# Retention and bilinear feed-forward on one core: weight pieces of 2, 3, 3 and 4 blocks, shared K^T V banks, first rows by thirds, one stretch moved

## The chip, the cores and the metric

The kernel runs on one core of a Trainium2 chip. The metric is the device time of one execution in microseconds (us), the median of several runs; lower is better. A profiled execution gives a trace beside it: PE is TensorE (matmul), PEld its weight load, DVE is VectorE, ACT is ScalarE, POOL is GpSimd, SP is SyncE, which issues most of the DMAs. L12 is line 12 of the kernel's file.

## What is computed

Retention over q, k, v (8 batches, 8 heads, 576 positions, 64 per head), with a decay gamma per head, and after it a bilinear feed-forward on the 4608 tokens, all in float32 outside of the chip:

```python
scores = scale * np.matmul(q, k.transpose(0, 1, 3, 2))
Dmat = np.where(rel >= 0, gamma[:, None, None] ** rel[None, :, :], 0.0)
attn = np.matmul(scores * Dmat[None], v)                  # B, H, S, D
x = attn.transpose(0, 2, 1, 3).reshape(B * S, H * D)      # 4608 x 512
out = ((x @ w_a) * (x @ w_b)) @ w_out                     # 512 -> 1536 -> 512
```

## The kernel before

**Retention in blocks of 64.** The tokens are handled in 18 pairs `n` of 256 tokens (the last 64 positions of each batch are gathered into two pairs of their own). Within a block of 64 positions, K Q^T is formed on PE ("scores", `sc`), masked to the causal part on DVE (`sT`) and multiplied with V ("keys"). What comes from earlier blocks goes through a state K^T V per head, summed over blocks: PE forms `kv`, DVE adds it up in `sums`, ACT converts the sums to bf16 `states`, and PE multiplies these with Q. The output `o` times the decay `qs` is `x`, written by DVE in bf16.

**Opening.** The first three pairs are handled in six steps (batch, half of the heads): step 0 and 2 make pair 0, steps 1 and 3 make pair 1, steps 4 and 5 (later) pair 2. A step casts Q and K to bf16 (`cast_step`, on an engine that is named), decays V (`values_step`), transposes Q and K on PE (`transpose_step`), forms scores (`score_step`) and K^T V (`state_step`: `state_products` on PE, then `state_copies` on ACT: `state_after`, which the second 128 tokens need, and the sums `own` and `second`, kept for later), and its output (`open_step`, `step_states`, `step_keys`, `close_step`; the last is the DVE product that writes x). The order is written out by hand in lines 858 to 934: each engine works through its own instructions in the order in which they stand there. PE fills waits with matmuls of ones (`warm`), which keep nothing.

**Weights.** `load_w` has POOL's queue cast columns of wa and wb from float32 to bf16 while loading them. `WCOLS` gives the pieces in blocks F of 128 columns, 3, 4 and 5 of the 12; wo follows in three thirds (`load_wo`). SP's later loads of q, k, v stand behind a small DMA (`gate`) that reads the first third of wo.

**Feed-forward.** `ffn_block` takes 512, 256, 256 and then 512 tokens at a time. For each F, four matmuls give `pa` (x wa), ACT copies it to `ha` in bf16, four give `pb` (x wb), and DVE multiplies the two into `hT`. In the first block the F are grouped as the weight pieces are: all pa of a piece, then all pb. The first piece's pa is begun early by `ffn_begin` on the first 256 tokens and by `begin_with` on the next. Then, for every 128 tokens u, twelve matmuls with wo give the rows `po`, which ACT or DVE copies to `osb`, and SP stores them; for the first three blocks the stores are held back (`held`).

**Banks.** `ps_ffn` is a pool of four PSUM banks with the tag "ab", shared by pa, pb, po, the transposes of the opening and two `kv` tiles of a stretch. A new tile waits for the last reader of the bank that it takes.

**Work in between.** `ffn_block` is a generator that yields a cost for each matmul (512 columns are 1). A list `todo` holds functions with due costs; the loop in lines 1029 to 1037 runs those that are due at the next edge (after a pb; after the 4th, 8th and 12th matmul of a row group). Block 0 runs from cost 0 to 144, block 1 to 216 (its two row groups from 192 and 204), block 2 to 288. `stretch(into, outof)` is such a function: it puts on PE the states part of pair `outof`, K^T V and the scores of pair `into`, and the keys of `outof`; an ACT copy `fence` stands between the first and the last. What follows on DVE and ACT is put on the list `later`: the adds of `sums` (in two parts for pairs in `SPLIT`), the two halves of x (`scaled`), and two entries that convert the sums on ACT (`convert`, `convert_swapped`) and mask the scores on DVE (`masked`). `pop()` in `ffn_block` issues one entry: after each pb, and in a row group after matmul 3, 6, 9 and at its end behind the `osb` copy. `flush()` at a block's end issues what is left, before the next block's first instruction. Each engine runs its instructions in the order of issue.

Of the kernel before, what the change touches and what calls it, by code (L numbers as in the profile page):

```python
# [18 lines left out]
def kernel(  # L19
# [25 lines left out]
    NP = NTOK // 256  # L45
    LEFT = {NP - 3: 0, NP - 1: 1}
    FIRST = 3
    SPLIT = (3, 5)
    assert S == 9 * 64 and B == 8

    PAIRS = [(0, 0), (1, 0), (2, 0), (0, 1), (1, 1), (2, 1)]
# [76 lines left out]
    def half(i):  # L128
        return slice(64 * i, 64 * i + 64)
# [132 lines left out]
    def load_w(f0, f1, which="ab"):  # L262
        if "a" in which:
            nc.gpsimd.dma_start(wa_sb[:, :, f0:f1], wa_r[:, :, f0:f1])
        if "b" in which:
            nc.gpsimd.dma_start(wb_sb[:, :, f0:f1], wb_r[:, :, f0:f1])
# [12 lines left out]
    def pop():  # L279
        if later:  # L280
            later.pop(0)()
# [28 lines left out]
    def cast_step(i, w, on):  # L310
        COPY[on](by_parity(natural[STEPS[i]][0][:, w]), given(i, w))  # L311
# [70 lines left out]
    def state_copies(i, kvs, rest=None):  # L382
# [12 lines left out]
        else:  # L395
            rest.append(keep)

    def total_of(n):

        own = own_sums[n]  # L400
        if n < FIRST - 1:
            nc.gpsimd.tensor_tensor(own, own, second[:, n], op=ALU.add)
            nc.gpsimd.tensor_copy(own_states[n], own)
        else:
            nc.vector.tensor_tensor(own, own, second[:, n], op=ALU.add)
            nc.scalar.copy(own_states[n], own)
        sums_of[n, 0] = own
# [266 lines left out]
    def close_outputs(n):  # L674

        o, begun = opened.pop(n)
        keys_into(n, o, begun)
        scaled = scaling(n, o)
        later.append(lambda: scaled(0))
        later.append(lambda: scaled(1))  # L680
# [33 lines left out]
    def stretch(into, outof):  # L714

        flush()
        if into == FIRST:
            ps_next("ps_pair")
        if into in LEFT:
            own = [ps_ffn.tile([128, HP, 2, 64], FP32, tag="ab", name=f"os{a}")  # L720
                   for a in (0, 1)]
            of_keys = ps_o[0].tile([128, 2, HP, 2, 64], FP32, tag="o",
                                   name="o2")
            from_states(outof, own, Begun())
            masked = matched(into)
            keys_into(outof, of_keys, Begun())
            summing(outof, own, of_keys)
            later.append(lambda: masked(0))
            later.append(lambda: masked(1))
            return  # L730
        if outof is not None:
            open_outputs(outof)
        convert, convert_swapped = keyed(into, outof is None)
        masked = matched(into)
        if outof is not None:
            close_outputs(outof)
        later.append(lambda: (convert(), masked(0)))
        later.append(lambda: (convert_swapped(), masked(1)))

    WCOLS = [3, 4, 5]  # L740

    def store(u, cols, osb):
        n, u = place(u // 2), u % 2
# [25 lines left out]
    def begin_with(F, c, m):  # L769
        begun[F, c, m] = True  # L770
        nc.tensor.matmul(begun[F][:, 256 * m:256 * m + 256],  # L771
                         wa_sb[:, c, F * 128:F * 128 + 128],
                         x_of(256 * m, 256)[:, c], start=(c == m == 0),
                         stop=(c == NC - 1), skip_group_check=True)

    def ffn_block(tb, tok0, n, runs):

        xT = x_of(tok0, n)
        hT = h_pool.tile([128, NF, 512], BF16, tag="h", name="hT")
        f0 = 0  # L780
        for count in runs:
            has = {}
            for F in range(f0, f0 + count):
                fs = slice(F * 128, (F + 1) * 128)
                pa = (begun[F] if tb == 0 and F in begun else
                      ps_ffn.tile([128, 512], FP32, tag="ab", name="pa"))
                for c in range(NC):
                    if tb == 0 and (F, 0, 0) in begun:
                        if (F, c, 1) not in begun:
                            begin_with(F, c, 1)  # L790
                        if c < NC - 1:
                            yield n / 512, False
                        continue
                    nc.tensor.matmul(pa[:, 0:n], wa_sb[:, c, fs],  # L794
                                     xT[:, c],
                                     start=(c == 0), stop=(c == NC - 1))
                    if c < NC - 1:
                        yield n / 512, False
                if n == 512 and tb:
                    pop()  # L800
                ha = ha_pool.tile([128, 512], BF16, tag="ha", name="ha")
                nc.scalar.copy(ha[:, 0:n], pa[:, 0:n])  # L802
                has[F] = ha
                yield n / 512, False
            for F in range(f0, f0 + count):
                fs = slice(F * 128, (F + 1) * 128)
                pb = ps_ffn.tile([128, 512], FP32, tag="ab", name="pb")
                for c in range(NC):
                    nc.tensor.matmul(pb[:, 0:n], wb_sb[:, c, fs],  # L809
                                     xT[:, c],  # L810
                                     start=(c == 0), stop=(c == NC - 1))
                    if c < NC - 1:
                        yield n / 512, False
                nc.vector.tensor_tensor(hT[:, F, 0:n], has[F][:, 0:n],  # L814
                                        pb[:, 0:n], op=ALU.mult)
                pop()
                yield n / 512, True
            f0 += count
        for u in range(n // 128):
            final = tok0 + (u + 1) * 128 == NTOK  # L820
            osb = o_pool.tile([128, DM], FP32, tag="osb", name="osb")
            edges = (0, DM // 2, 3 * DM // 4, DM) if final else (0, DM)
            for part in range(len(edges) - 1):
                cols = slice(edges[part], edges[part + 1])
                po = ps_ffn.tile([128, 512], FP32, tag="ab", name="po")
                width = cols.stop - cols.start
                for F in range(NF):
                    nc.tensor.matmul(po[:, 0:width],  # L828
                                     hT[:, F, u * 128:(u + 1) * 128],
                                     wo_sb[:, F, cols],  # L830
                                     start=(F == 0), stop=(F == NF - 1))
                    if F in (2, 5, 8):
                        pop()
                    if F < NF - 1:
                        yield width / 512, F % 4 == 3
                if n == 256 or (u + part) % 2 == 0:
                    nc.scalar.copy(osb[:, cols], po[:, 0:width])  # L837
                else:
                    nc.vector.tensor_copy(osb[:, cols], po[:, 0:width])  # L839
                if tb < 3:  # L840
                    held.append((tok0 // 128 + u, cols, osb))
                else:
                    store(tok0 // 128 + u, cols, osb)
                pop()
                yield width / 512, True
# [5 lines left out]
    def warm(count, n):  # L851

        w = ps_ffn.tile([128, 512], FP32, tag="ab", name="w")
        for _ in range(count):
            nc.tensor.matmul(w[:, 0:n], ones[:, 0:128], ones[:, 0:n],  # L855
                             start=True, stop=True)

    W1, W2 = 128 * WCOLS[0], 128 * (WCOLS[0] + WCOLS[1])
    vector, pool_ = nc.vector, nc.gpsimd
    warm(8, 512)  # L860
    make_qs(qs_o, 0, 0, 256)
# [18 lines left out]
    warm(2, 512)  # L880
    transpose_step(2, (K, "dve"))
    warm(2, 512)
    load_w(0, W1, "a")
    cast_step(1, Q, "act")
    score_step(2)
    transpose_step(1, (K, "act"))
# [2 lines left out]
    values_step(2, 1, pool_)  # L889
    values_step(2, 0, pool_)  # L890
    make_qs(qs_o, 3, 0, 256)
    load_w(0, W1, "b")
    warm(2, 512)
    score_step(1)
    cast_step(3, Q, "act")
    state_step(2)
    cast_step(3, K, "pool")
    warm(2, 512)
    transpose_step(3, (Q, "act"))
    transpose_step(3, (K, "dve"))  # L900
# [2 lines left out]
        values_step(1, kp, pool_)  # L903
    values_step(3, 0, nc.scalar)
    values_step(3, 1, pool_)
    load_w(W1, W2)
    score_step(3)
    rest = []
    state_step(1, rest)
    state_step(3, rest)  # L910
    for keep in rest:
        keep()
    open_step(1)
    step_keys(1, {0, 1})
    step_states(1, False)
    close_step(1)
    open_step(3, ps_sc)
    step_keys(3, {0, 1})
    step_states(3, False)
    close_step(3)  # L920
    for F in range(3):
        ffn_begin(F)
    for c in (0, 1):
        for F in range(3):
            begin_with(F, c, 1)
    load_w(W2, DFF)
    for i in (0, 1, 2):
        load_wo(i)
    make_masks()
# [54 lines left out]
    def third_turn():  # L984
        for i in (4, 5):
# [6 lines left out]
    todo += [(60 + 10 * n, total_of, (n,)) for n in (0, 1)]  # L992
    todo += [(136, total_of, (2,))]
    todo += [(28 + 6 * step, pair_tables, (step,)) for step in range(13)]
    todo += [(170, stretch, (3, None)), (197, stretch, (4, 3)),
             (252, stretch, (5, 4)), (274, open_alone, (5,)),
             (278, close_outputs, (5,)), (336, stretch, (6, None)),
             (372, stretch, (7, 6)), (408, stretch, (8, 7))]
# [69 lines left out]
```

## Time and profile before

| | us |
|---|---|
| median of 3 runs | 325.16 (325.08 to 325.69) |
| the profiled execution | 325.43 |
| its span, first to last instruction | 323.7 |
| busy: PE, DVE, ACT, POOL | 314.0, 165.4, 131.5, 118.8 |
| first matmul of the feed-forward (L771) starts | 16.81 |
| first rows with wo (L828) start | 37.57 |
| block 1's last rows to block 2's first pa (chain) | 68.61 |
| last PE matmul done (chain) | 320.9 |

The span is that of the profiled execution; what lies around it (325.43 - 323.7) is launch and end. In the timelines each row is start, duration, engine, line, operation, output <- input, shape and count; rows of one form that follow each other are merged. In the chain of waits a row is start, duration and what the end was waiting for.

### The profile page before, as it was taken

The numbers are of one execution on the slowest core, as the hardware profiler recorded it, in microseconds if no ns is written. First come the engines' busy times: TensorE is split into PE (matmuls) and PEld (weight loads), VectorE is DVE, ScalarE is ACT, GpSimd is POOL, SyncE is SP. The second block draws the span as 40 slices with busy tenths as digits, with TensorE's granted clock in tenths as the row PEclk, the third lists the DMA queues.
The fourth block names the chain that finished last, engine by engine and source line by source line (L and its number), as shares of the span: only waits on it lengthen the run. The fifth ranks groups of instructions, "written<-read, shape, count | busy, mean of one in ns | idle before, by whom it ended". The sixth has DMA issues, their size and how long they took to land.

```text
span 323.7 us, 8631 instructions
## 1 busy us (share of the span) xinstructions
PE 314.0 (97%) x3573; PEld 164.4 (51%) x3611; DVE 165.4 (51%) x294; ACT 131.5 (41%) x293; POOL 118.8 (37%) x158
## 2 busy tenths in 40 slices
PE   7899999999999999999999999999999999999996
PEld 3564457778444554444454545454445444444444
DVE  5744445665546754835374626562566256514321
ACT  7735753463435523533253324442433343313321
POOL 4990077574755274447165305450530000000000
PEclk9999999999999999999999999999999999999999
DMA  8999999999999999999999169935840520031013
GB/s 216 255 196 207 259 231 189 200 176 206 174 221 223 195 208 206 269 222 263 175 197 216 52 163 198 207 74 144 194 86 19 104 76 2 2 97 32 1 23 108
DMA packets 145431, 50.90 MB, mean 157 GB/s; under 512 B 126704, under 2 KB 140912, under 8 KB 145392
## 3 DMA queue, kind: packets, MB, share of 16 engines
q1 hardware_dynamic: 140112, 45.37, 68.4%
q0 software_dynamic: 4752, 4.72, 8.8%
q8 instruction: 28, 0.46, 0.6%
q10 hardware_dynamic: 528, 0.26, 0.3%
q14 instruction: 11, 0.09, 0.1%
HBM read 37.75 MB, written 9.44 MB: 146 GB/s over the span
## 4 chain that ended last, share of the span: by engine, by line
PE 92%; DMA 2%; SPq 2%; ACT 1%; issue 1%; DVE 1%; DVEq 0%
PE pb L809 29%; PE po L828 29%; PE pa L794 28%; DMA qf<-in_q_dram 2%; SPq L159 2%; PE sc L600 1%; PE o L628 1%; PE o L641 1%; PE kv L538 1%; PE pa L771 1%; ACT state_after L386 0%; ACT vb L319 0%; PE tp L329 0%; DVE hT L814 0%; ACT own L390 0%
## 5 line engine op out<-in xcount | busy, mean ns | idle before, releaser
L814 DVE TENSOR_TENSOR hT<-ha,pb 128x512 bf16<-128x512 bf16 (+1 forms) x120 | 75.9, 633 | 94.8 <-PE pb L809 86.6
L802 ACT CAST ha<-pa 128x512 bf16<-128x512 f32 (+1 forms) x120 | 64.8, 543 | 115.9 <-PE pa L794 109.9
L809 PE MATMUL pb<-xT,wb_sb 128*128 128x512 bf16 (+1 forms) x474 | 111.2, 357 | 0.5
L794 PE MATMUL pa<-xT,wa_sb 128*128 128x512 bf16 (+1 forms) x452 | 106.9, 356 | 1.2 <-issue 0.6
L828 PE MATMUL po<-wo_sb,hT 128*128 128x512 bf16 (+2 forms) x442 | 94.7, 367 | 1.7 <-issue 1.4
L809 PEld LDWEIGHTS <-wb_sb 128*128 128x128 bf16 x480 | 47.0, 98 | 46.6 <-issue 0.3
L794 PEld LDWEIGHTS <-wa_sb 128*128 128x128 bf16 x468 | 45.0, 98 | 44.4 <-issue 0.2
L828 PEld LDWEIGHTS <-hT 128*128 128x128 bf16 x456 | 42.7, 98 | 47.2
L484 POOL CAST qkb<-qf 64x1024 bf16<-64x1024 f32 x15 | 15.5, 1031 | 64.4 <-DMA qf<-in_q_dram 55.1
L495 POOL TENSOR_TENSOR vb<-vf,vs 128x1024 bf16<-128x1024 f32 (+1 forms) x17 | 28.9, 1700 | 13.3 <-DMA vf<-in_v_dram 6.1
L839 DVE COPY osb<-po 128x512 f32<-128x512 f32 (+2 forms) x17 | 11.1, 653 | 43.0 <-PE po L828 43.0
L837 ACT COPY osb<-po 128x512 f32<-128x512 f32 (+1 forms) x21 | 12.0, 573 | 43.4 <-PE po L828 40.5
L484 POOL CAST qkb<-kf 64x1024 bf16<-64x1024 f32 (+1 forms) x17 | 16.4, 966 | 16.7 <-DMA kf<-in_k_dram 16.5
L563 DVE TENSOR_TENSOR sums<-kv,sums 128x256 f32<-128x256 f32 x44 | 18.7, 424 | 2.8 <-PE kv L538 0.8
L609 DVE TENSOR_TENSOR sT<-sc,mask 128x512 bf16<-128x512 f32 x30 | 19.4, 681 | 0.0
L488 POOL CAST qkb<-kf 64x512 bf16<-64x512 f32 (+1 forms) x34 | 18.7, 579 | 1.0
L488 POOL CAST qkb<-qf 64x512 bf16<-64x512 f32 x30 | 17.6, 615 | 0.6
L567 ACT CAST states<-sums 64x512 bf16<-64x512 f32 x26 | 16.0, 617 | 0.3
L654 DVE TENSOR_TENSOR xT<-o,qs 128x512 bf16<-128x512 f32 x24 | 15.4, 682 | 1.5 <-PE o L641 1.5
L311 POOL CAST qkb<-kf 128x512 bf16<-128x512 f32 x5 | 3.1, 617 | 16.9 <-DMA kf<-in_k_dram 16.9
L355 DVE TENSOR_TENSOR sT<-sc,mask_s 128x1024 bf16<-128x1024 f32 x6 | 7.2, 1222 | 1.3 <-PE sc L347 1.2
L855 PE MATMUL w<-ones 128*128 128x512 bf16 x17 | 6.3, 482 | 1.5 <-DVE idxp_f L204 1.5
(88 smaller groups left out, 163.5 us busy)
## 6 DMA issues: line engine op xcount, KB each, us to landing
qf<-in_q_dram SPq DMA_DIRECT2D x32, 256.0 KB, 4.7
vf<-in_v_dram SPq DMA_DIRECT2D x32, 256.0 KB, 5.2
kf<-in_k_dram SPq DMA_DIRECT2D x31, 256.0 KB, 4.8
out_dram<-osb SPq DMA_DIRECT2D x25, 256.0 KB, 3.2
out_dram<-osb SPq DMA_DIRECT2D x21, 128.0 KB, 2.6
wo_sb<-in_moe_w_out_dram POOLq DMA_DIRECT2D x3, 512.0 KB, 16.7
qf<-in_q_dram SPq DMA_DIRECT2D x8, 128.0 KB, 3.2
kf<-in_k_dram SPq DMA_DIRECT2D x8, 128.0 KB, 3.5
```

What stands on the lines that cost most here:

```text
L484: nc.gpsimd.tensor_copy(qkb[0:64, w, e], t[0:64, e])
L488: nc.gpsimd.tensor_copy(to[:, :, 1 - r], fro[:, :, r])
L495: nc.gpsimd.tensor_tensor(vb[:, e].rearrange("p (h d) -> p h d", d=D), t[:, e].rearrange("p (h d) -> p h d", d=D), decay[:, at], op=ALU.mult)
L563: nc.vector.tensor_tensor(sums[:, i], own, prev, op=ALU.add)
L567: nc.scalar.copy(to(half(1 - r)), fro(half(r)))
L609: nc.vector.tensor_tensor(sT[:, on].rearrange("p c k s -> p (c k) s"), sc[:, on].rearrange("p c k s -> p (c k) s"), mask3.unsqueeze(1).to_ ...
L654: nc.vector.tensor_tensor(x_of(t0, 128).rearrange("p c (a s) -> p c a s", a=2), o[:, :, :, kp].rearrange("p a c s -> p c a s"), qs[:, :, s ...
L794: nc.tensor.matmul(pa[:, 0:n], wa_sb[:, c, fs], xT[:, c], start=(c == 0), stop=(c == NC - 1))
L802: nc.scalar.copy(ha[:, 0:n], pa[:, 0:n])
L809: nc.tensor.matmul(pb[:, 0:n], wb_sb[:, c, fs], xT[:, c], start=(c == 0), stop=(c == NC - 1))
L814: nc.vector.tensor_tensor(hT[:, F, 0:n], has[F][:, 0:n], pb[:, 0:n], op=ALU.mult)
L828: nc.tensor.matmul(po[:, 0:width], hT[:, F, u * 128:(u + 1) * 128], wo_sb[:, F, cols], start=(F == 0), stop=(F == NF - 1))
```

## The change

It does five things. (1) The weights come in pieces of 2, 3, 3 and 4 blocks, so the first block groups its F in this way and begins two of them early instead of three; wa's second piece is issued on POOL right behind wb's first, ahead of the values of steps 1 and 3, and wb's second where both stood. The cast of K in step 3 goes from POOL to DVE, ahead of the mask of step 1. (2) `last_states` forms K^T V of steps 1 and 3 in two shared banks and copies both steps together, four ACT copies instead of eight; the outputs follow as keys, keys, states, states and then both DVE products. (3) `rows_together` forms the first two row groups of block 0 side by side, four blocks of wo at a time. (4) `stretch(4, 3)` is due at cost 201 instead of 197. (5) Pair 4's adds are split in two, and the second part is put behind the two halves of x.

```diff
--- before.py
+++ after.py
@@ -45,7 +45,7 @@
     NP = NTOK // 256
     LEFT = {NP - 3: 0, NP - 1: 1}
     FIRST = 3
-    SPLIT = (3, 5)
+    SPLIT = (3, 4, 5)
     assert S == 9 * 64 and B == 8
 
     PAIRS = [(0, 0), (1, 0), (2, 0), (0, 1), (1, 1), (2, 1)]
@@ -394,6 +394,22 @@
             keep()
         else:
             rest.append(keep)
+
+    def last_states():
+
+        own, later_half = kvs = [
+            ps_ffn.tile([128, 2, 2, 64], FP32, tag="ab", name=f"kv1{a}")
+            for a in (0, 1)]
+        fresh = set(QUADS)
+        for i in (1, 3):
+            state_products(i, [kv[:, i // 2] for kv in kvs], fresh)
+        for r in (0, 1):
+            nc.scalar.copy(state_after[half(r), 1, :, half(r)],
+                           own[half(r)].rearrange("p i j d -> p (i j) d"))
+        nc.scalar.copy(own_sums[1],
+                       own.rearrange("p i j d -> p (i j) d"))
+        nc.scalar.copy(second[:, 1],
+                       later_half.rearrange("p i j d -> p (i j) d"))
 
     def total_of(n):
 
@@ -734,10 +750,12 @@
         masked = matched(into)
         if outof is not None:
             close_outputs(outof)
+        if into == 4:
+            later.append(later.pop(1))
         later.append(lambda: (convert(), masked(0)))
         later.append(lambda: (convert_swapped(), masked(1)))
 
-    WCOLS = [3, 4, 5]
+    WCOLS = [2, 3, 3, 4]
 
     def store(u, cols, osb):
         n, u = place(u // 2), u % 2
@@ -772,6 +790,28 @@
                          wa_sb[:, c, F * 128:F * 128 + 128],
                          x_of(256 * m, 256)[:, c], start=(c == m == 0),
                          stop=(c == NC - 1), skip_group_check=True)
+
+    def rows_together(tok0, hT, us):
+
+        pos = [ps_ffn.tile([128, 512], FP32, tag="ab", name="po") for _ in us]
+        for f0 in range(0, NF, 4):
+            for u, po in zip(us, pos):
+                for F in range(f0, f0 + 4):
+                    nc.tensor.matmul(po, hT[:, F, u * 128:(u + 1) * 128],
+                                     wo_sb[:, F], start=(F == 0),
+                                     stop=(F == NF - 1))
+                    if F < NF - 1:
+                        yield 1, F % 4 == 3
+                pop()
+                if f0 + 4 < NF:
+                    continue
+                osb = o_pool.tile([128, DM], FP32, tag="osb", name="osb")
+                if u % 2 == 0:
+                    nc.scalar.copy(osb, po)
+                else:
+                    nc.vector.tensor_copy(osb, po)
+                held.append((tok0 // 128 + u, slice(0, DM), osb))
+                yield 1, True
 
     def ffn_block(tb, tok0, n, runs):
 
@@ -816,7 +856,9 @@
                 pop()
                 yield n / 512, True
             f0 += count
-        for u in range(n // 128):
+        if tb == 0:
+            yield from rows_together(tok0, hT, (0, 1))
+        for u in range(2 if tb == 0 else 0, n // 128):
             final = tok0 + (u + 1) * 128 == NTOK
             osb = o_pool.tile([128, DM], FP32, tag="osb", name="osb")
             edges = (0, DM // 2, 3 * DM // 4, DM) if final else (0, DM)
@@ -855,7 +897,8 @@
             nc.tensor.matmul(w[:, 0:n], ones[:, 0:128], ones[:, 0:n],
                              start=True, stop=True)
 
-    W1, W2 = 128 * WCOLS[0], 128 * (WCOLS[0] + WCOLS[1])
+    edges = [128 * sum(WCOLS[:i]) for i in range(len(WCOLS) + 1)]
+    pieces = list(zip(edges, edges[1:]))
     vector, pool_ = nc.vector, nc.gpsimd
     warm(8, 512)
     make_qs(qs_o, 0, 0, 256)
@@ -880,7 +923,7 @@
     warm(2, 512)
     transpose_step(2, (K, "dve"))
     warm(2, 512)
-    load_w(0, W1, "a")
+    load_w(*pieces[0], "a")
     cast_step(1, Q, "act")
     score_step(2)
     transpose_step(1, (K, "act"))
@@ -889,12 +932,13 @@
     values_step(2, 1, pool_)
     values_step(2, 0, pool_)
     make_qs(qs_o, 3, 0, 256)
-    load_w(0, W1, "b")
+    load_w(*pieces[0], "b")
+    load_w(*pieces[1], "a")
     warm(2, 512)
+    cast_step(3, K, "dve")
     score_step(1)
     cast_step(3, Q, "act")
     state_step(2)
-    cast_step(3, K, "pool")
     warm(2, 512)
     transpose_step(3, (Q, "act"))
     transpose_step(3, (K, "dve"))
@@ -903,27 +947,23 @@
         values_step(1, kp, pool_)
     values_step(3, 0, nc.scalar)
     values_step(3, 1, pool_)
-    load_w(W1, W2)
+    load_w(*pieces[1], "b")
     score_step(3)
-    rest = []
-    state_step(1, rest)
-    state_step(3, rest)
-    for keep in rest:
-        keep()
-    open_step(1)
-    step_keys(1, {0, 1})
-    step_states(1, False)
-    close_step(1)
-    open_step(3, ps_sc)
-    step_keys(3, {0, 1})
-    step_states(3, False)
-    close_step(3)
-    for F in range(3):
+    last_states()
+    for i, banks in ((1, None), (3, ps_sc)):
+        open_step(i, banks)
+        step_keys(i, {0, 1})
+    for i in (1, 3):
+        step_states(i, False)
+    for i in (1, 3):
+        close_step(i)
+    for F in range(WCOLS[0]):
         ffn_begin(F)
     for c in (0, 1):
-        for F in range(3):
+        for F in range(WCOLS[0]):
             begin_with(F, c, 1)
-    load_w(W2, DFF)
+    for piece in pieces[2:]:
+        load_w(*piece)
     for i in (0, 1, 2):
         load_wo(i)
     make_masks()
@@ -992,7 +1032,7 @@
     todo += [(60 + 10 * n, total_of, (n,)) for n in (0, 1)]
     todo += [(136, total_of, (2,))]
     todo += [(28 + 6 * step, pair_tables, (step,)) for step in range(13)]
-    todo += [(170, stretch, (3, None)), (197, stretch, (4, 3)),
+    todo += [(170, stretch, (3, None)), (201, stretch, (4, 3)),
              (252, stretch, (5, 4)), (274, open_alone, (5,)),
              (278, close_outputs, (5,)), (336, stretch, (6, None)),
              (372, stretch, (7, 6)), (408, stretch, (8, 7))]
```

## The prediction

> **What bounds the kernel.** Read first: the page's engine line, then the chain of waits, then the timelines of the two places that the diff touches (8 to 21 us and 60 to 76 us), then the DMA issues.
>
> ```profile
> PE 314.0 (97%) x3573; PEld 164.4 (51%) x3611; DVE 165.4 (51%) x294; ACT 131.5 (41%) x293; POOL 118.8 (37%) x158
> ```
>
> TensorE is idle 9.7 of 323.7 us. In the table of 1 us windows nearly all of it lies before 16.8 us and in the 2.5 us of last store; from 16.8 us to 320.9 us PE is busy 95 to 100% of almost every window at clock 1.00. The change removes no matmul, so it can gain only by letting the feed-forward start before 16.81 us, and every new wait of PE behind that is paid in full. PE in the opening (start, duration), then ACT and DVE at the same time:
>
> ```profile
> 15.70 0.32 PE L437 MATMUL o<-sT,vb 64*64 64x128 bf16 x9 [0.25 <-issue]
> 15.96 0.28 PE L421 MATMUL o<-qkT,state_after 128*128 128x128 bf16 x2
> 16.17 0.42 PE L437 MATMUL o<-sT,vb 64*64 64x128 bf16 x16
> 16.52 0.29 PE L421 MATMUL o<-qkT,state_after 128*128 128x128 bf16 x2
> 16.81 2.79 PE L771 MATMUL pa<-xT,wa_sb 128*128 128x256 bf16 x24
> ```
> ```profile
> 14.93 1.08 ACT L386 CAST state_after<-kv 64x128 bf16<-64x128 f32 x4
> ```
> ```profile
> 14.64 1.21 DVE L355 TENSOR_TENSOR sT<-sc,mask_s 128x1024 bf16<-128x1024 f32 x1
> ```
>
> The reader should see that step 3's mask ends at 15.85, that L771 follows the last L421 without a gap, and that four state copies end at 16.01. The DMA issues (KB written, us from issue to landing):
>
> ```profile
> wa_sb<-in_moe_w_a_dram POOLq DMA_DIRECT2D x1, 640.0 KB, 10.6
> wb_sb<-in_moe_w_b_dram POOLq DMA_DIRECT2D x1, 640.0 KB, 13.1
> wa_sb<-in_moe_w_a_dram POOLq DMA_DIRECT2D x1, 512.0 KB, 7.0
> wb_sb<-in_moe_w_b_dram POOLq DMA_DIRECT2D x1, 512.0 KB, 8.2
> ...
> wa_sb<-in_moe_w_a_dram POOLq DMA_DIRECT2D x1, 384.0 KB, 7.7
> wb_sb<-in_moe_w_b_dram POOLq DMA_DIRECT2D x1, 384.0 KB, 7.1
> ```
>
> Added to their issues on the POOL timeline (wa 9.07, 14.78, 16.31; wb 11.56, 15.58, 17.05) they land at 16.77, 18.66, 21.78, 23.78, 26.91 and 30.15 us, with 384, 768, 1280, 1792, 2432 and 3072 KB there by then. The first landing also sits at PE's start: the weight load of L771 is shown waiting 0.2 us for it.
>
> **Opening, the pieces.** The first piece is 256 KB instead of 384, so by the stream's 200 KB/us it lands about 0.6 us earlier (near 16.1) and no longer holds PE. For a start S = 16.6, PE needs 512 KB at 18.5 (16 half-width matmuls at 0.116, from 24 in 2.79), 896 KB at 20.2 (8 of L809 at 0.216), 1280 KB at 22.8, 1664 at 25.4, 2048 at 28.0, 2560 at 30.6, 3072 at 34.0. Read off the landings in proportion, these amounts are there at 17.4, 19.4, 21.8, 23.3, 25.0, 27.6 and 30.2. Least slack 0.8 us: cost 0, taken as -0 to +0.4 because the 512 KB piece at 21.78 came 0.6 us behind the proportion. Two more DMA issues on POOL (0.77 each) stand before wo and the masks; with the K cast gone (0.62) POOL ends its opening near 21.9, and the first index table that DVE wants from it is due near 23.7: hidden.
>
> **Opening, the cast and the moved issue.** wa's second piece now stands ahead of step 1's values on POOL: 0.81 in, 0.62 of K cast out, so values shift by under 0.2 us; ACT's own values of step 3 (until 15.04) still end last. DVE is free from 11.50 (x of step 0 written) to 11.88; K of step 3, landing between its neighbours in the SP queue (V of step 2 at 10.43, Q of step 3 at 12.07), about 11.3, costs 0.43 there and pushes the mask of step 1 by about 0.05 us, which nothing reads before 15.13. Cost 0.
>
> **Opening, shared banks.** Eight ACT copies of 128 columns (14.93 to 16.81) become four of 256. They now wait for step 3's products, whose last matmul ends at 15.34. A 128x256 copy out of PSUM is 0.37 us (L802's 256 form), so the two state copies end near 16.1. PE meanwhile does the keys of step 1, then of step 3 (mask done 15.85; 16 matmuls take 0.35 before the next), then all four state matmuls (0.31 in the block of four at 48.06 to 48.37): 15.9 + 0.35 + 0.31 = 16.56 at best. With the 0.25 us issue hole at 15.45 kept, keys of step 1 end at 15.96 and S is 16.62. Against 16.81 that is -0.19 to -0.25; I take **-0.2**, bounds -0.3 (nothing can pass the mask) and 0 (the hole grows, or the x of step 3, due 17.9 and wanted 18.0 now that two blocks are begun instead of three, comes 0.1 to 0.2 late).
>
> **First rows by thirds.** Same 24 matmuls, same banks (four: po, po and two free), copies still one on ACT and one on DVE. The last third of wo lands at 38.1 (issue 19.2 + 18.9), was wanted at 39.3 (37.57 + 8 x 0.216), is now wanted at 40.9. It was not late before: 0. Row 0's copy moves 0.8 us later, and on ACT now precedes the Q cast of step 5, which PE's transposes want at 43.4; done by 42.9, so hidden, bounds 0 to +0.2.
>
> **The later stretch.** Stretch(4, 3), due 197, ran at cost 200, after the 8th matmul of block 1's first rows; due 201 it runs at 204, after the 12th. What it defers is popped at matmuls 3, 6, 9 and the end of a row group. Before: adds and first x half still in rows 0, second x half, then both conversions inside rows 1. Now only four pops are left in rows 1, and with the adds cut in two and the second half put last they are add, x, x, add. The conversions are emitted by the flush behind the block, **behind the copy of rows 1 and ahead of block 2's first ha copy** on ACT. ACT and the chain before:
>
> ```profile
> 66.06 0.59 ACT L837 COPY osb<-po 128x512 f32<-128x512 f32 x1 [1.66 <-PE po L828]
> 66.67 0.41 ACT L570 CAST states<-sums 128x256 bf16<-128x256 f32 x1
> 67.08 1.25 ACT L567 CAST states<-sums 64x512 bf16<-64x512 f32 x2
> 68.34 0.82 ACT L567 CAST left_states<-sums 64x256 bf16<-64x256 f32 x2
> 69.06 0.57 ACT L837 COPY osb<-po 128x512 f32<-128x512 f32 x1
> 69.54 0.84 ACT L802 CAST ha<-pa 128x256 bf16<-128x256 f32 x2
> ```
> ```profile
> 65.21 3.40 PE po L828 x15
> 68.61 0.44 PE pa L794 x4
> ...
> 70.36 0.44 PE pa L794 x4
> ```
>
> DVE stays in time: adds begin 0.86 later (65.45), two adds 0.9, two x halves 1.28, so x is complete near 67.7 as before (66.38 + 1.28) and block 2 can start at 68.65; the last two adds end at 68.5, before pb wants their bank at 68.9. ACT does not. It idles through rows 1, copies them from 68.66 (start to start 0.61), then L570 0.41, L567 1.26, left_states 0.72, all read off the start times above: the first ha begins at 71.66 and ends at 72.03. PE has four banks: pa, pb, pa, pb of block 2 fill them, 4 x 0.44 = 1.75 us, until 70.41; the next pa needs the bank that the first ha copy empties, and every other bank waits behind that copy too (hT reads ha). Before, that copy ended at 69.91, 0.45 ahead of need; now it is 72.05 - 70.4 = **1.65 us** late. Behind it hT, pb and pa follow in step, as ha copies come each 0.47 us against PE's 0.88 a pair. Bounds: 1.3 (each of the spacings 0.07 shorter) to 2.0 (hT's turn and the wake-up add to it). Nothing later gives it back: PE has no idle time that waits on absolute time (DMA) behind this point.
>
> **Sum.** 325.43 is the profiled execution's time with span 323.7 in it; -0.2 + 1.65 = +1.45 gives span 325.15 and 326.9 for that execution. The median of the runs shown is 325.16, 0.27 below it, so **326.6**. The likeliest case's own range, by its bounds: 326.1 to 327.3.
>
> **Rivals.**
> (a) *Not slower*: ACT's queue is not what PE waits for. It would take conversions issued inside rows 1, or under 1.35 us of them in front of the first ha, so that it ends before 70.4. For: ACT is 41% busy and before had 0.45 us to spare. Against: the emission order and its one queue. Then only the opening counts: 325.16 - 0.2 = 324.95, at most 324.85.
> (b) *Half a stall*: the copies run closer together and the next bank is free sooner, say half of 1.65: 325.8. Against: their start times are back to back already.
> (c) *The stream falls behind*: each of the two pieces added holds the weights up by as much as a 384 KB piece took (18.66 - 16.77 = 1.9 us): the last third of wo lands at 41.9 against 40.9, 1.0 more: 327.6. Against: time per KB is 1.89/384, 3.13/640 and 3.24/640, 4.9 to 5.1 ns for every size, which leaves no fixed part. The Trainium skill, page "DMA: Bandwidth & Descriptors", section "Rules for kernel authors", speaks against the cut: it wants transfers of 1 MiB or more, and "Anatomy of one DMA" fits about 2.0 us fixed per DMA. By that, an estimate from that page, the two pieces would cost 4.0 us of stream, wo's last third 42.1, and the time 327.85. These landings show no such part where transfers queue behind one another.
>
> **Chances.** Forecast 0.80, (a) 0.09, (b) 0.06, (c) 0.05. A measurement of this kernel tells 0.2% (0.65 us) from no change: below 324.5 is faster, above 325.8 slower. (a) lies within, with a third of it for an opening that gains more than I can find; (b) on the bound, half to each. Faster 0.04, same 0.09, slower 0.87. The range leaves out (a), most of (c) and the tails: 325.7 to 327.4.
>
> **What will show it.** In the profile after: L771's successor starts near 16.6 with no DMA wait; no PE wait between 17 and 43; near 68 us ACT shows osb, states, left_states, ha in that order, and PE a gap of 1.6 us before block 2's third pa, the longest after the opening. No gap there makes the prediction wrong; a gap before F 2 or in the first rows makes (c) right.

## The result, and the profile after

| | before | changed |
|---|---|---|
| median, us (6 runs each) | 325.14 | 327.34 (327.19 to 328.04) |
| ratio to before | | 1.0066, 95% interval 1.0054 to 1.0079 |
| the profiled execution, and its span | 325.43, 323.7 | 327.38, 325.7 |
| first pa of the feed-forward starts | 16.81 | 16.67 |
| first rows with wo start | 37.57 | 37.53 |
| block 2's third pa starts | 70.19 | 72.06 |
| scores of stretch(5, 4) start | 76.93 | 78.80 |
| copy of the last rows (DVE) starts | 320.90 | 322.84 |

The changed kernel is 2.2 us slower. The table places the loss: nothing until the first rows, 1.87 us at block 2's third pa, and 1.94 us at the end. From that pa to the end the distance moves by no more than 0.1 us. ACT's timeline of the changed kernel around block 1's end (start, duration, line, what; in brackets the idle time before and its releaser):

```profile
64.66 0.58 ACT L879 COPY osb<-po 128x512 f32<-128x512 f32 x1 [1.44 <-PE po L870]
65.14 0.17 ACT L687 COPY fence<-o 128x2 f32<-128x2 f32 x1
68.64 0.58 ACT L879 COPY osb<-po 128x512 f32<-128x512 f32 x1 [3.34 <-PE po L870]
69.25 0.41 ACT L586 CAST states<-sums 128x256 bf16<-128x256 f32 x1
69.67 1.25 ACT L583 CAST states<-sums 64x512 bf16<-64x512 f32 x2
70.93 0.82 ACT L583 CAST left_states<-sums 64x256 bf16<-64x256 f32 x2
71.65 0.62 ACT L842 CAST ha<-pa 128x256 bf16<-128x256 f32 x2
```

And PE at the same time:

```profile
68.44 0.60 PE L834 MATMUL pa<-xT,wa_sb 128*128 128x256 bf16 x4
68.88 0.60 PE L849 MATMUL pb<-xT,wb_sb 128*128 128x256 bf16 x4
69.32 0.60 PE L834 MATMUL pa<-xT,wa_sb 128*128 128x256 bf16 x4
69.75 0.60 PE L849 MATMUL pb<-xT,wb_sb 128*128 128x256 bf16 x4
72.06 0.60 PE L834 MATMUL pa<-xT,wa_sb 128*128 128x256 bf16 x4 [1.71 <-ACT ha L842]
72.50 0.60 PE L849 MATMUL pb<-xT,wb_sb 128*128 128x256 bf16 x4
```

In the kernel before, the third pa followed without a wait:

```profile
69.76 0.60 PE L809 MATMUL pb<-xT,wb_sb 128*128 128x256 bf16 x4
70.19 0.60 PE L794 MATMUL pa<-xT,wa_sb 128*128 128x256 bf16 x4
```

ACT stands idle for 3.34 us while the second row group is formed, then copies its rows and runs the five conversions before the first ha copy. PE fills its four banks, pa, pb, pa, pb, and stops until that copy is done. DVE isn't what holds them: its last mask ends at 69.55, and it then waits for the same ha copy:

```profile
72.04 0.75 DVE L854 TENSOR_TENSOR hT<-ha,pb 128x256 bf16<-128x256 bf16 x2 [2.50 <-ACT ha L842]
```

In the view of waits PE's stop is the longest of the whole execution:

```profile
PE pa L834 <- ACT ha L842: 1.7, 1, 1.7
PE w L897 <- DVE idxp_f L204: 1.5, 1, 1.5
PE sc L347 <- ACT qkT L333: 0.5, 2, 0.3
PE o L453 <- DVE sT L355: 0.2, 1, 0.2
PE kv L374 <- POOL vb L321: 0.2, 1, 0.2
```

The other four lie before 16.7 us. There is none for a weight and none in the first rows; the list names none below 0.2 us. The opening of the changed kernel on PE:

```profile
15.24 0.30 PE L374 MATMUL kv<-vb,qkb 64*64 64x64 bf16 x12 [0.20 <-POOL vb L321]
15.35 0.52 PE L453 MATMUL o<-sT,vb 64*64 64x128 bf16 x16
16.08 0.42 PE L453 MATMUL o<-sT,vb 64*64 64x128 bf16 x16 [0.21 <-DVE sT L355]
16.43 0.40 PE L437 MATMUL o<-qkT,state_after 128*128 128x128 bf16 x4
16.67 2.03 PE L789 MATMUL pa<-xT,wa_sb 128*128 128x256 bf16 x16
```

The keys of step 3 wait for its mask, as worked out; the values' later place on POOL is also seen, as a wait of 0.20 us that the mask hides. One short wait follows. The begun pa need the x of step 3 from their thirteenth matmul on, and DVE writes both x products last:

```profile
16.76 1.29 DVE L464 TENSOR_TENSOR xT<-o,qs_o 128x512 bf16<-128x512 f32 x2 [0.73 <-PE o L437]
```

They end at 18.05, and PE starts the thirteenth matmul at 18.10, 0.23 us after the twelfth where the others stand 0.11 apart. So 0.10 of the 0.14 that the earlier first pa had gained is gone by the first rows (20.86 us from the one to the other, against 20.76 before).

### The profile page after: what moved, and what is told of

Its sections match the earlier page's. It is cut to its first block, busy times and chain, and to the rows that moved or that the text cites. A ratio compares the mean times of both kernels' runs of the same rounds, so it can differ in the third digit from the quotient of the medians.

```text
span 325.7 us, 8659 instructions
## 1 busy us (share of the span) xinstructions
PE 318.3 (98%) x3607; PEld 164.3 (50%) x3607; DVE 166.0 (51%) x295; ACT 130.9 (40%) x289; POOL 118.9 (37%) x159
## 4 chain that ended last, share of the span: by engine, by line
PE 93%; ACT 2%; DVE 2%; DMA 1%; SPq 1%; issue 1%; DVEq 0%
PE pb L849 28%; PE pa L834 28%; PE po L870 26%; PE po L800 2%; PE w L897 1%; PE sc L616 1%; PE o L657 1%; PE o L644 1%; DMA vf<-in_v_dram 1%; PE kv L554 1%; PE tp L329 1%; SPq L148 1%; PE pa L789 1%; PE sc L347 1%; DVE sums L579 0%
## 5 line engine op out<-in xcount | busy, mean ns | idle before, releaser
L834 PE MATMUL pa<-xT,wa_sb 128*128 128x512 bf16 (+1 forms) x472 | 109.8, 357 | 1.7 <-ACT ha L842 1.7
L870 PE MATMUL po<-wo_sb,hT 128*128 128x512 bf16 (+2 forms) x432 | 91.8, 367 | 0.0
L870 PEld LDWEIGHTS <-hT 128*128 128x128 bf16 x432 | 40.4, 98 | 44.3
L881 DVE COPY osb<-po 128x512 f32<-128x512 f32 (+2 forms) x16 | 10.4, 649 | 39.0 <-PE po L870 38.9
L897 PE MATMUL w<-ones 128*128 128x512 bf16 x19 | 7.4, 513 | 1.5 <-DVE idxp_f L204 1.5
```

Of the source, the lines that this page charges most:

```text
L834: nc.tensor.matmul(pa[:, 0:n], wa_sb[:, c, fs], xT[:, c], start=(c == 0), stop=(c == NC - 1))
L870: nc.tensor.matmul(po[:, 0:width], hT[:, F, u * 128:(u + 1) * 128], wo_sb[:, F, cols], start=(F == 0), stop=(F == NF - 1))
```

## The experiments

Theory: all of the loss is the place of pair 4's conversions in ACT's queue. Rivals: the opening takes part of it; the kv banks, freed late by the split adds; the stretch's place itself. The first four kernels ran together beside the kernel before (median 325.43 over 24 runs), and so did the last three (325.21 over 21).

**e1, the opening alone.** Start from the changed kernel (here and below, lines without a change are left out between the pieces):

```diff
-    SPLIT = (3, 4, 5)
+    SPLIT = (3, 5)
-        if into == 4:
-            later.append(later.pop(1))
-    todo += [(170, stretch, (3, None)), (201, stretch, (4, 3)),
+    todo += [(170, stretch, (3, None)), (197, stretch, (4, 3)),
```

> The changed kernel with stretch(4, 3) due at 197 again and pair 4's adds in one piece and in their old place: only the opening and the first rows by thirds are left of the change. Theory (all of the loss is ACT's queue behind block 1): 325.0 to 325.2, the gain of the opening being at most 0.25 us and 0.05 by the one profile of the changed kernel; no PE gap near 70 us. Rival (the opening itself costs part of the 2.2 us): 325.5 or more.

Measured 325.23 (11 runs), ratio 0.9997 (0.9979 to 1.0014), and no PE wait in the list after the opening. The loss of 2.2 us is not in the opening or the rows by thirds. The interval (0.7 us faster to 0.5 slower) is too wide to tell a small gain or cost of theirs.

**e2, the later stretch alone.** Start from the kernel before:

```diff
-    todo += [(170, stretch, (3, None)), (197, stretch, (4, 3)),
+    todo += [(170, stretch, (3, None)), (201, stretch, (4, 3)),
```

> The kernel before with one number changed: stretch(4, 3) due at 201. Theory: the conversions go behind the copy of rows 1, PE waits about 1.7 us for block 2's third pa, and the time is 1.9 above before: 327.0. Rival (the loss needs the new opening too, or the split adds): under 1 us above before, below 326.1.

Measured 327.56 (4 runs, 327.29 to 329.89), ratio 1.0078 (1.0051 to 1.0105). PE's timeline:

```profile
69.52 0.60 PE L794 MATMUL pa<-xT,wa_sb 128*128 128x256 bf16 x4
72.14 0.60 PE L794 MATMUL pa<-xT,wa_sb 128*128 128x256 bf16 x4 [1.59 <-ACT ha L802]
```

One number is enough for the loss, with the old opening and the old adds. The profiled execution took 327.29, near the 327.0 expected; the median of four is raised by the others, one of them 329.89.

**e3, the same place, conversions behind block 2's first products.** Start from the changed kernel; `convert_left` is the part of `convert_swapped` that writes `left_states`, and `behind` is added to `later` behind the flush at the block's end (the lines for that are left out here):

```diff
+        if into == 4:
+            behind.extend([lambda: (convert(), masked(0)), convert_swapped,
+                           lambda: masked(1), convert_left])
+            return
```

> The changed kernel, stretch at 201 and adds split as in the change; only pair 4's two conversions and masks are issued one by one behind block 2's first four pb instead of ahead of its first pa. Theory (what PE waits for is the first ha copy, behind five ACT instructions): the gap at the third pa goes, at most 0.3 us of short waits in its place, 325.1 to 325.4. Rival (the kv banks, held by the adds that now come last, or the stretch's place itself): the 1.9 us stay, 327.

Measured 325.33 (12 runs), ratio 0.9995 (0.9978 to 1.0013). ACT:

```profile
68.65 0.59 ACT L886 COPY osb<-po 128x512 f32<-128x512 f32 x1 [3.30 <-PE po L877]
69.14 0.37 ACT L849 CAST ha<-pa 128x256 bf16<-128x256 f32 x1
69.54 0.41 ACT L587 CAST states<-sums 128x256 bf16<-128x256 f32 x1
70.02 0.37 ACT L849 CAST ha<-pa 128x256 bf16<-128x256 f32 x1
```

The stretch is at 201, the adds are split and end as late as in the change, the same instructions run, and the wait is gone. That rules out the kv banks and the place itself. The masks on DVE move with the conversions, but the result section shows that DVE was waiting for ha, not PE for DVE. Against e1 in the two profiles it ends 0.55 us later from a first pa that is 0.28 later; 0.10 of these 0.27 us is lost by the next stretch, the rest further on; what takes them was not looked for. The medians differ by 0.10.

**e4, the split adds alone.** Start from the kernel before, stretch at 197, with the two edits on pair 4's adds from the change.

> The kernel before, stretch at 197, but pair 4's adds split with the second part behind the two halves of x, as in the change. Theory: one entry more in the list puts the swapped conversions (1.26 and 0.72 us) behind the copy of rows 1, so the first ha ends near 71.6 instead of 69.9 and PE waits 1.2 us, 1.4 with its restart: 326.5. Rival (only the later stretch costs): 325.1.

Measured 326.58 (5 runs), ratio 1.0033 (1.0020 to 1.0046):

```profile
66.45 0.41 ACT L570 CAST states<-sums 128x256 bf16<-128x256 f32 x1
68.42 0.59 ACT L839 COPY osb<-po 128x512 f32<-128x512 f32 x1 [1.57 <-PE po L830]
69.04 1.25 ACT L567 CAST states<-sums 64x512 bf16<-64x512 f32 x2
70.29 0.82 ACT L567 CAST left_states<-sums 64x256 bf16<-64x256 f32 x2
71.02 0.63 ACT L804 CAST ha<-pa 128x256 bf16<-128x256 f32 x2
```

One entry more in the list moves four of the five conversions behind the copy, and PE waits 1.30 us. The medians differ by 1.15. So each of the two edits is enough by itself; together they are not worse than the later place alone, as that one already puts all five there.

**e5 and e6, only a longer queue.** Start from the kernel before; six copies, or one, at the end of block 1, into a tile `spare` that nothing reads:

```diff
         flush()
+        if tb == 1:
+            for _ in range(6):
+                nc.scalar.copy(spare, qs_o[:, 0])
         tok += n
```

> The kernel before with six extra ACT copies of 128 x 256 (float32 to bf16, about 0.41 us from start to start) issued at the end of block 1, ahead of block 2's first ha copy. Theory (four banks give 1.75 us, the first ha copy had 0.45 us to spare, then every delay is paid one to one with 0.2 for the restart of PE): that copy ends 2.5 later, PE waits about 2.0 us, 327.3. Rival (PE waits for the kv banks or for x, not for ha): 325.2.

> The same with one such copy. Theory: 0.41 us fits into the 0.45 to spare, no PE wait: 325.1 to 325.3. Rival (any ACT work there costs its length): 325.6.

One copy: 325.30 (10 runs), ratio 1.0011 (1.0001 to 1.0021). No PE wait is listed, but the third pa started 0.20 us late in its profile, at 70.08 where 0.44 behind the pb is 69.88:

```profile
69.44 0.60 PE L810 MATMUL pb<-xT,wb_sb 128*128 128x256 bf16 x4
70.08 0.60 PE L795 MATMUL pa<-xT,wa_sb 128*128 128x256 bf16 x4
```

So there is a cost where none was expected: 0.09 us by the medians, 0.20 in the profile. The interval, 0.03 to 0.7 us, holds the rival's 0.4 too, so the times alone don't decide; the profile shows half of the copy's length. The slack was smaller than the 0.45 that the expectation took from the prediction: before, the first ha copy ended at 69.91 and the third pa started at 70.19, which leaves 0.28.

Six copies: 329.2 (4 runs, 327.28 to 330.10), ratio 1.0116 (1.0085 to 1.0146), where 327.3 was expected. PE's wait is 2.22 us, where about 2.0 was, and only the lowest run is at the expected time. The windows of the profiled execution (330.10) show a part of the rest for that one:

```profile
core 0: us, PE busy (x) PEld busy (x) DVE busy (x) ACT busy (x) POOL busy (x), PEclk, DMA share, GB/s
70.00:73.20 3.20, 0.98 (x10) 0.73 (x9) 0.03 (x1) 3.02 (x9) 3.03 (x6) 1.00 0.80 135
73.20:75.00 1.80, 1.80 (x14) 1.52 (x14) 1.14 (x3) 0.71 (x3) 1.06 (x2) 0.82 0.85 164
75.00:77.00 2.00, 2.00 (x12) 1.39 (x10) 0.42 (x1) 0.62 (x2) 0.00 (x0) 0.50 1.19 236
77.00:79.00 2.00, 2.00 (x16) 1.67 (x15) 0.81 (x2) 0.39 (x2) 0.00 (x0) 0.81 0.79 172
```

The column PEclk is the granted clock. PE starts again at 73.19; from 74.3 to 77.8 the clock is 0.50, and there PE starts a group of four matmuls each 0.86 us instead of 0.44, a loss of some 1.7 us. This execution's first pa also started late, at 17.34. The run of 328.69 shows a mean clock of 1.000 and stays unexplained. ACT work alone, with no bank, x or stretch changed, makes the wait of 2.22 us.

**e7, the same place, conversions ahead of the copy.** Start from the changed kernel, adds in one piece (that edit is as in e1):

```diff
         if into == 4:
+            adds, one, two = later
+            later[:] = [adds, lambda: (one(), two()),
+                        lambda: (convert(), convert_swapped()),
+                        lambda: (masked(0), masked(1))]
+            return
```

> The changed kernel with the stretch at 201, pair 4's adds in one piece, and the list worked off as adds, both x halves, both conversions within rows 1, so that the conversions stand ahead of the copy of rows 1 on ACT; the masks go last. Theory (the order of issue costs, not the place of the stretch): conversions end near 69.1, rows 1's copy near 69.7, the first ha copy near 70.0 before it is needed at 70.4: no PE wait, 325.1 to 325.3. Rival (the later place itself costs): 326.5 or more. The start of the feed-forward, 16.43 to 16.88 in six profiles so far, tells with this one and the other two whether the old opening's hole of 0.25 us before its last keys belongs to it.

Measured 325.33 (11 runs), ratio 1.0004 (0.9995 to 1.0013), no PE wait at block 2. ACT in the profiled execution, which started its feed-forward 0.7 us later than the changed kernel's:

```profile
68.85 0.82 ACT L583 CAST left_states<-sums 64x256 bf16<-64x256 f32 x2
69.58 0.57 ACT L883 COPY osb<-po 128x512 f32<-128x512 f32 x1
70.05 0.36 ACT L846 CAST ha<-pa 128x256 bf16<-128x256 f32 x1
```

The order of issue costs, not the place. No kernel of these beats the one before: the intervals of e1, e3 and e7 hold a ratio of 1.

## Why the prediction was right

**The later stretch, right in mechanism, sized 0.2 low.** ACT's five instructions came to the prediction's times within 0.02 us (first ha at 71.65 against 71.66; PE again at 72.06 against 72.05). What was off is the time at which PE wanted the bank. The prediction took the end of the fourth group, 70.41; but groups that follow each other overlap, 0.60 us long and started 0.44 apart, so the third pa was due to start at 70.19, as it did before. From there to 72.06 is 1.87, of which the list of waits shows the 1.71 behind the end of the fourth group. The same step gave the slack of 0.45 that e6 found to be 0.28. e2, e3, e5 and e7 show the cause by removing and by making it.

**The split adds.** The prediction gave them no price of their own, since the later stretch hides it; e4 shows that they cost by themselves in the old place 1.15 by the medians, and 1.46 in its profile from the start that was due (69.53 + 0.44) to 71.43.

**The opening, -0.2 predicted, nothing found.** Two things are off. The first is the base: 16.81, with the issue hole of 0.25 us before step 1's last keys counted as part of the old order. It comes and goes. The same old opening started the feed-forward at 16.48 in e4 and at 16.44 in e6, without the hole:

```profile
15.15 0.60 PE L437 MATMUL o<-sT,vb 64*64 64x128 bf16 x16
15.68 0.29 PE L421 MATMUL o<-qkT,state_after 128*128 128x128 bf16 x2
15.90 0.42 PE L437 MATMUL o<-sT,vb 64*64 64x128 bf16 x16
16.25 0.28 PE L421 MATMUL o<-qkT,state_after 128*128 128x128 bf16 x2
16.48 0.72 PE L773 MATMUL pa<-xT,wa_sb 128*128 128x256 bf16 x5
```

The new one's best, in e1, is 16.43. In both, step 3's keys wait for its mask; the old order forms step 1's states during that wait, so forming all states behind the keys gains nothing there. The hole shows in two of five profiles of the old opening (that of the kernel before and e2's) and in none of four of the new; whether the new order avoids it is not shown. The five start at 16.44 to 17.34, the four at 16.43 to 17.40, so e1's comparison, uncertain by 0.6 us, can't tell a gain of 0.05. The second is the late x of step 3, which the prediction had among its bounds for this term: it costs 0.10 in every profile of the new opening, 20.86 us from first pa to first rows in all four, against 20.75 to 20.76 in all five of the old.

**The weights and the thirds, cost 0: right.** No PE wait for a weight. The first pieces landed at 15.87 (9.27 + 6.6) and 17.14 (11.74 + 5.4), against about 16.1 and 17.4 worked out. The last third of wo landed at 38.4 (20.32 + 18.1), against 38.1 before and the 41.9 of rival (c). The case that the stream falls behind is refuted here. The Trainium skill's rule on transfer size ("DMA: Bandwidth & Descriptors", "Rules for kernel authors") has no price in this kernel: eight pieces of 256 to 512 KB fed PE as six did. One argument against (c) was read too well: "4.9 to 5.1 ns for every size" leaves out the two pieces of 512 KB, which by the prediction's own landings took 6.1 and 3.9 ns per KB. Whether the thirds would help with a later wo wasn't tried.

**The sum.** -0.2 + 1.65 gave 326.6. Between the two profiles it is -0.14 at the first pa, 0.10 for x, 0.03 up to block 2, 1.88 for the wait and 0.07 behind it, 1.94 in all. The medians differ by 2.2; the 0.26 left is of the size by which runs of one kernel differ. Both terms were off in the same direction, and 327.34 lies 0.06 inside the range's upper end of 327.4: that the range holds it is partly luck, the mechanism is not. Rival (a) also had a wrong condition: the conversions last 0.41 + 1.26 + 0.72 = 2.39 us and made the first ha copy 1.65 late, so no wait needed under 0.74 us of them there, not under 1.35.

## What to carry to other kernels

When work is put off to a list, ask where the list is emptied: the last entries land ahead of the next stage's first copies on the same engine, and until those copies PE can only fill the banks that are free. Here that was 1.75 us of matmul against 3.4 us of ACT work, on an engine that is 41% busy. Measure the slack from the start at which PE is due, not from the end of what it does before. Before a saving is counted from a gap in one profile, look whether the gap is there in another of the same code; and compare the distance between two starts over all profiles, which here shows a loss of 0.10 us that no list of waits names.

## What was not expected of the hardware

In e5's profile 3.4 us at a granted clock of 0.50 came 1.2 us behind a PE wait of 2.22 us, and two of four executions had a mean clock of 0.995 and took 329.7 and 330.1 us. So had one of four in e2 (329.89; the wait is 1.59 in its profiled execution, which kept a clock of 1.000), and none of six of the changed kernel (1.71). That the wait is the cause is not shown: of the kernel before, which has no such wait, 2 of 24 executions beside e1 to e4 also had 0.995 and took 328.28 and 328.53, though none of 21 beside e5. The Trainium skill, page "TensorE: Matmul & The Clock Gate", section "Why this matters for your kernels", asks for no idle gaps above about 3 us. In e5's profile the clock fell with no gap longer than 2.22 us. At the start, two of the filling matmuls took 1.06 us in the changed kernel and 0.59 before:

```profile
5.95 1.06 PE L897 MATMUL w<-ones 128*128 128x512 bf16 x2
```
```profile
5.58 0.59 PE L855 MATMUL w<-ones 128*128 128x512 bf16 x2
```

The code up to there is the same, and the row of that window shows clock 1.00 in both; the cause stays open. Part of the scatter of the opening goes with it: in the three profiles in which the eight transposes just ahead took 1.05 to 1.06 us (the changed kernel, e3, e5; 0.80 to 0.99 in the others), step 3's mask started at 14.81 to 14.85, in the other six at 14.56 to 14.64. In e5 and e7, the two that started after 17.3, ACT waited for V of step 3 until 14.97, where before it began on it at 13.96.
